# Layer norms in pairs, eight turns in one PSUM bank, and a new order for a two-layer attention and GLU kernel

## The chip, the cores and the metric

The kernel runs on one core of a Trainium2 chip. The metric is the device time of one execution in microseconds; the median of several runs is compared. The engines are named as in the profile: PE (TensorE, matmuls), PEld (its weight loads), DVE (VectorE), ACT (ScalarE), POOL (GpSimd) and SP (SyncE, which here issues most DMAs).

## The reference, cut to what matters

The input x has 2048 tokens of 512 numbers in bf16. Two layers are computed, with the same weights. Each has a sliding-window attention (32 heads of 16, window 256) and a gated feed-forward part (hidden size 1792), each on a layer norm of x and added to x:

```
def _layernorm(x, axis=-1, eps=1e-5):
    m = jnp.mean(x, axis=axis, keepdims=True)
    v = jnp.var(x, axis=axis, keepdims=True)
    return (x - m) / jnp.sqrt(v + eps)
...
    mask = (idx[:, None] - idx[None, :] >= 0) & (idx[:, None] - idx[None, :] < W)
    scores = jnp.where(mask[None, None], scores, -1e9)
    p = _softmax(scores, axis=-1)
    o = jnp.einsum("bhqk,bhkd->bhqd", p, v)
...
    h = _sigmoid(g) * u
    return jnp.einsum("bsf,fd->bsd", h, w_down)
...
x = x + _A_ref(_layernorm(x, axis=-1), A_wqkv, A_wo)
x = x + _B_ref(_layernorm(x, axis=-1), B_w_gate, B_w_up, B_w_down)
```

The last two lines are done twice. `A_x` is the input; `B_x` is not used.

## The kernel before, in words

The tokens are cut into 16 tiles of 128, and the tiles into four groups of four. x lies in SBUF for the whole run (`xsb`), and so do all weights.

**A norm.** `layer_norm` makes tasks for one tile. DVE takes the statistics (`stats`, L600 and L602), POOL adds epsilon and takes the inverse root (`root`, L612 and L613), DVE applies them (`apply`, L629) into a buffer `xn`, of which there are four, one tile each. PE turns the tile's four 128 x 128 blocks with the identity (L647) into one PSUM bank, as bf16, and ACT or DVE copies the bank (L676 is ACT's copy and L678 DVE's, both in a helper `copy`) into `xnT`, which holds a group of four tiles. There are 64 norms: per layer 16 for the attention (kind "p") and 16 for the feed-forward part (kind "g").

**The attention.** Q (L713), K (L744, with a split by VectorE at L759) and V (L780) are matmuls of a group or a tile. Scores go into four PSUM banks (`Sps`, L1039, L1050, L1060) in visits; each visit ends in one exponential on ACT of up to 128 x 2048 (L1092), and DVE multiplies with masks (L970). The values (L1119) go half a tile at a time into a bank; the result is moved to SBUF (`OTs`), transposed on DVE (`turn`, L1138), divided by the sums (`norm`, L1144 and L1146), and transposed back (`turn2`, L1151). The output projection (L903) adds to x (L909) and starts the feed-forward norm of the tile.

**The feed-forward part.** Tiles are taken in groups of 1, 2 or 4, in the lists `GLU`; `OPT["g0"]` picks the list of layer 0 (always followed by two groups of 4) and `OPT["g2"]` that of layer 1. A unit fills one bank with gate and up matmuls (L808; 128 columns wide for a group of one, 512 for four, where gate and up have a bank each), ACT takes the tanh (L826), DVE multiplies (L834), and the down projection (L872) ends with an addition to x on DVE (L881), which starts the next layer's norm or the store. Four PSUM banks (`BANKS`) are shared by all that isn't scores.

**The order.** It is fixed when the kernel is built. A planner written in Python keeps a clock, a queue of tasks for each engine and a list of open units for PE. A task has a duration in ns for each engine that can do it and a priority from `PRIO` (lower goes first); where two engines can do it, the one that would end it earlier takes it. A PE unit is chosen by `RANK`. `PACE` sets the least distance of score visits, with other values for the first `EARLY` visits, and from visit `PACE[4]` on `LATE_PRIO`, `LATE_RANK` and `LATE_SLACK` hold. The instructions are written out in the order in which the planner starts them, so each engine's own order is that of the plan, and the hardware waits with semaphores. The durations and priorities make no instruction longer or shorter; they set order and engine. In the plan, DVE's copy of a turned tile has 152 + 512/0.96 + 100 ns; the turn has 1130, the norm 1030, the second turn 600. When PE has nothing to do, the planner may put in idle-filling matmuls (L1257).

`OPT["bk"]` and `OPT["bq"]` are the numbers of first K and Q units that work tile by tile, 128 columns wide. `OPT["hold"]` makes the third and fourth norm wait for earlier ones. `OPT["g1"]` is used only by the changed kernel.

The lines that name the buffers and the tasks of a norm:

```
        ring("xn", 4, [P, 1, D])
...
        b = pl.task({"POOL": 800 - 230 * first}, root, [a.done], self.prio["st_" + kind])
        c = pl.task({"DVE": 406}, apply, [b.done], self.prio["ap_" + kind], can, port=True)
...
            d = pl.task({"ACT": act_ns(KT * P), "DVE": dve_ns(KT * P) + 100}, lambda e: self.copy(
                e, self.xnT[key][0][:, i], pt), [u.done], self.prio["tp" if key[0] == "p" else "tp_g"])
```

Of the kernel before, what the change touches and what calls it, by code (L numbers as in the profile page):

```python
# [9 lines left out]
ALU = mybir.AluOpType  # L10
# [34 lines left out]
def act_ns(n):  # L45
    return 171 + n / 1.2


def dve_ns(n):
    return 152 + n / 0.96  # L50
# [6 lines left out]
def pool_ns(n):  # L57
# [2 lines left out]

EXP_NS = 1880
TAIL = (384, 128)
GLU = [[[1, 1, 1, 1, 2, 2], [1, 1, 1, 1, 2, 2], [1, 1, 2, 2, 2], [1, 1, 1, 1, 1, 1, 1, 1], [2, 2, 2, 2], [1, 1, 1, 1, 1, 1, 1, 1], [2, 2, 4]], [[4, 4, 4, 4], [4, 4, 4, 2, 1, 1], [4, 4, 2, 1, 1, 4]]]
PACE = [2681.81, 1328.37, 1196.7, 872.42, 21.95]
EARLY = 16
FILL = 800
OVERLAP = {"ACT": 114, "DVE": 83, "POOL": 45, "SP": 0}
LATENCY = {"ACT": 45, "DVE": 40, "POOL": 60, "SP": 0}
# [11 lines left out]
FETCH = (1200, 2300)  # L80


PRIO = dict(st_x0=8.026, ap_x0=7.059, xt_x0=10.785, st_x1=3.545, ap_x1=6.693, xt_x1=8.977, st_x=12.044,
    ap_x=12.327, xt_x=-6.634, st_p=-1.733, ap_p=4.349, xt_p=1.138, st_g=-6.356, ap_g=3.74, xt_g=-5.594,
    st_g0=3.292, ap_g0=-10.915, xt_g0=-4.847, tp=7.272, tp_g=6.212, q=-0.67, q0=11.129, q1=-22.989,
    k=-9.747, k0=14.768, k1=0.61, s=-5.3, s0=4.016, s1=2.634, v=0.444, v0=23.378, v1=20.074, vv=-6.331,
    exp=-13.785, exp0=-0.049, m0=3.46, m00=4.795, e0=-8.802, e00=0.423, e1=-0.562, e10=9.011, m2=-6.041,
    m20=0.716, th=15.676, mu=-10.778, dn=-20.12, add=2.096, add0=7.831, out=-15.994, mv=31.961, mv0=5.964,
    oq=-8.579, oq0=-11.733, no=13.392, no0=-3.279, on=11.451, on0=-10.714, vc=11.541, vc0=-1.273)
OPT = dict(gu='SP', g1=0, bk=3, bq=3, wide=0, r0=2, g0=5, g2=0, x0=1, eps=1, hold=1, own=1, ck=0, cq=2,  # L90
    turn=2, split=0, mo=0, at=3, r1=3, near=3)
SLACK = dict(xt=5595, oq=812, on=1665, vc=730)
RANK = dict(tp=-16.462, o=-6.977, lead=17.162, far=65.44, v=20.015, g=58.528, d=32.436, feed=40.797,
    x3=34839.477, wd=1492.629, go=176.096)
LATE_PRIO = dict(st_p=-4.956, ap_p=38.034, xt_p=0.962, st_x=-1.619, ap_x=-5.199, xt_x=17.448, st_g=-14.573,
    ap_g=-6.614, xt_g=0.299, q=-17.247, k=34.931, s=-1.549, v=-6.237, exp=-43.312, m0=4.641, e0=8.453,
    e1=11.689, m2=17.496, th=2.747, mu=-20.998, dn=2.523, add=-6.022, out=27.029, mv=45.566, oq=-5.883,
    no=8.561, on=11.817, vc=-20.116)
LATE_SLACK = dict(xt=541, oq=5451, on=4000, vc=10531)
LATE_RANK = dict(tp=52.672, o=-17.659, lead=2.057, far=12.106, v=-5.627, g=-3.049, d=10.813, feed=-60.763,  # L100
    go=344.346)

# [28 lines left out]
def when_all(events, fn):  # L133
    left = [e for e in events if not e.fired]
    if not left:
        fn()
        return
    count = [len(left)]

    def one():  # L140
        count[0] -= 1
        if count[0] == 0:
            fn()

    for e in left:
        e.waiting.append(one)
# [226 lines left out]
class Net:  # L373


    def __init__(self, ctx, tc, A_x, wqkv, wo, w_gate, w_up, w_down, out):
# [41 lines left out]
        def ring(name, n, shape, dt=BF16):  # L418
            self.bufs[name] = [[big.tile(shape, dt, name=f"{name}{i}"), True] for i in range(n)]

        ring("xn", 4, [P, 1, D])
        ring("xnT", 3, [P, NBG, KT, P])
        ring("OTs", 1, [P, 8, P])
        ring("Oq", 1, [P, 8, P])
# [161 lines left out]
    def layer_norm(self, key, t, deps):  # L586

        nc, pl = self.nc, self.pl
        done = self.xn_ready[key, t]
        box = {}  # L590
        kind = "x" + ("0" if key[2] == 0 else "1" if key[2] == 1 else "") if key[:2] == ("p", 0) else (
            "p" if key[0] == "p" else "g0" if key[1] * NT + t < 4 else "g")

        first = key == ("p", 0, 0) and OPT["eps"]

        def stats(e):
            if "st" not in box:
                box["st"] = self.take("st")
            st = box["st"][0][:, 0]
            nc.vector.bn_stats(out=st[:, 0:6], in_=self.xsb[:, t, :])  # L600
            if not first:
                nc.vector.bn_aggr(out=st[:, 6:8], in_=st[:, 0:6])  # L602

        def moments(e):
            st = box["st"][0][:, 0]
            nc.vector.bn_aggr(out=st[:, 6:8], in_=st[:, 0:6])
            nc.vector.tensor_scalar(out=st[:, 9:10], in0=st[:, 7:8], scalar1=1e-5, scalar2=None, op0=ALU.add)

        def root(e):
            st = box["st"][0]  # L610
            if not first:
                nc.gpsimd.tensor_scalar(out=st[:, 0, 9:10], in0=st[:, 0, 7:8], scalar1=1e-5, scalar2=None, op0=ALU.add)  # L612
            nc.gpsimd.tensor_tensor(out=st[:, 0, 8:9], in0=st[:, 0, 9:10], in1=self.nhalf[:, 0:1], op=ALU.pow)  # L613

        def can():
            if not self.has("xn"):
                return False
            if key in self.xnT:
                return True
            room = sum(b[1] for b in self.bufs["xnT"])  # L620
            mine = sum(k[0] == key[0] for k in self.xnT)
            return room > 0 and (mine == 0 or room > 1 or key[:2] == ("p", 0))

        def apply(e):
            box["xn"] = b = self.take("xn")
            if key not in self.xnT:
                self.xnT[key] = self.take("xnT")
            st = box["st"][0][:, 0]
            nc.vector.tensor_scalar(out=b[0][:, 0, :], in0=self.xsb[:, t, :], scalar1=st[:, 6:7], scalar2=st[:, 8:9],  # L629
                                    op0=ALU.subtract, op1=ALU.mult)  # L630

        if key == ("p", 0, 0) and t >= 2 and OPT["hold"]:
            deps = deps + [self.applied[t - 2]]
        a = pl.task({"DVE": 694 if first else 910}, stats, deps, self.prio["st_" + kind], lambda: "st" in box or self.has("st"))
        if first:
            a = pl.task({"DVE": 390}, moments, [a.done] + ([self.applied[t - 1]] if 0 < t <= OPT["mo"] else []), self.prio["ap_" + kind] + 0.1)
        b = pl.task({"POOL": 800 - 230 * first}, root, [a.done], self.prio["st_" + kind])
        self.roots[key + (t,)] = b.done
        c = pl.task({"DVE": 406}, apply, [b.done], self.prio["ap_" + kind], can, port=True)
        c.done.then(lambda: self.give(box["st"]))  # L640
        if key == ("p", 0, 0):
            c.began_ev = self.applied[t]
        i = t % NBG
        def steps(bank):
            pt = self.tp_view(bank)
            xn = box["xn"][0][:, 0]
            return [(57, lambda c=c: nc.tensor.transpose(pt[:, c, :], xn[:, c * P:(c + 1) * P], self.ident[:]))  # L647
                    for c in range(KT)]

        def evac(u):  # L650
            pt = self.tp_view(u.bank)
            if key == ("p", 0, 0) and t < OPT["split"]:
                half, both = KT // 2, Event()
                when_all([pl.task({e: ns}, lambda e, o=o: self.copy(e, self.xnT[key][0][:, i][:, o:o + half], pt[:, o:o + half]), [u.done],
                                  self.prio["tp"] - 9).done for e, ns, o in (("ACT", act_ns(half * P), 0), ("DVE", dve_ns(half * P) + 50, half))], both.fire)
                both.then(lambda: (self.give(box["xn"]), done.fire()))
                return both
            d = pl.task({"ACT": act_ns(KT * P), "DVE": dve_ns(KT * P) + 100}, lambda e: self.copy(
                e, self.xnT[key][0][:, i], pt), [u.done], self.prio["tp" if key[0] == "p" else "tp_g"])
            d.done.then(lambda: (self.give(box["xn"]), done.fire()))  # L660
            return d.done

        def ready():
            u = Unit(("tp", t), steps, [], False, evac)
            if key == ("p", 0, 0) and OPT["own"]:
                u.own = BANKS + t
            self.streams[0].append(u)

        c.done.then(ready)

    def tp_view(self, bank, n=KT):
        return self.banks[bank][:, 0:n * P // 2].bitcast(BF16).rearrange("p (c q) -> p c q", c=n)
# [452 lines left out]
    def after_values(self, L, t, half, bank, done):  # L1125
# [29 lines left out]
        a.done.then(lambda: self.release(bank))  # L1155
        if half == 0:
            return
        b = pl.task({"DVE": 1130}, turn, [box[0], box[1]], self.prio["oq0" if early else "oq"], lambda: self.has("Oq"), port=True)
        b.done.then(lambda: self.give(box["OTs"]))
        c = pl.task({"DVE": 1030}, norm, [b.done], self.prio["no0" if early else "no"], lambda: self.has("On"), port=True)  # L1160
        c.done.then(lambda: (self.give(box["Oq"]), self.give(box["Rt"])))
        d = pl.task({"DVE": 600}, turn2, [c.done], self.prio["on0" if early else "on"], lambda: self.has("OnT"), port=True)

        def landed():
            self.give(box["On"])
# [321 lines left out]
```

## Time and profile before

| what | value |
|---|---|
| median of 3 runs | 565.57 us (565.51 to 566.4) |
| the profiled execution's own time | 566.81 us |
| its span, first to last instruction | 565.1 us |
| granted PE clock | 1.00 in all slices |
| ACT, exponentials (122 + 32) | 226.7 + 56.9 us |
| PE, gate and up matmuls | 125.7 + 125.6 us |
| DVE, feed-forward products (140) | 78.0 us |
| DMA | 17.38 MB, 31 GB/s on average |

The profile is of one execution. A row of a group reads: line, engine, operation, output <- inputs, shapes, count | busy time in us, mean ns of one | idle time of the engine just before them, and what ended it. A row of the stages gives the stretch in us from the span's start, its length, busy us (and count) of PE, PEld, DVE, ACT and POOL, the granted clock, the busy share of the DMA engines, and GB/s. A row of the waits gives who waited <- for whom: us in total, times, longest. A row of the timeline gives start, duration, engine, line, operation and count of merged instructions, and in brackets the idle time before it. Matmuls overlap, so the distance from start to start tells their rate, not the duration.

### The profile page before, as it was taken

The numbers are of one execution on the slowest core, as the hardware profiler recorded it, in microseconds if no ns is written. First come the engines' busy times: TensorE is split into PE (matmuls) and PEld (weight loads), VectorE is DVE, ScalarE is ACT, GpSimd is POOL, SyncE is SP. The second block draws the span as 40 slices with busy tenths as digits, with TensorE's granted clock in tenths as the row PEclk, the third lists the DMA queues.
The fourth block names the chain that finished last, engine by engine and source line by source line (L and its number), as shares of the span: only waits on it lengthen the run. The fifth ranks groups of instructions, "written<-read, shape, count | busy, mean of one in ns | idle before, by whom it ended". The sixth has DMA issues, their size and how long they took to land.

```text
span 565.1 us, 22076 instructions
## 1 busy us (share of the span) xinstructions
PE 548.7 (97%) x9998; PEld 300.0 (53%) x9998; DVE 461.9 (82%) x921; ACT 407.8 (72%) x424; POOL 61.4 (11%) x153
## 2 busy tenths in 40 slices
PE   8999899999999999999999999999999999999997
PEld 7446565854788645444444444544444444544443
DVE  6999999999988899996699986989768999852332
ACT  3999989979999887891699827999189985530330
POOL 4411111111101120101100011000100001000000
PEclk9999999999999999999999999999999999999999
DMA  8723000000000000000000000000100000000001
GB/s 254 294 92 106 3 24 2 23 3 23 4 23 3 23 3 23 23 2 1 11 2 23 3 13 11 2 23 3 40 20 2 23 3 31 12 1 20 19 0 38
DMA packets 18574, 17.38 MB, mean 31 GB/s; under 512 B 1841, under 2 KB 17457, under 8 KB 18481
## 3 DMA queue, kind: packets, MB, share of 16 engines
q1 hardware_dynamic: 17360, 14.93, 8.1%
q8 instruction: 78, 1.28, 0.9%
q10 hardware_dynamic: 1120, 1.05, 0.6%
q14 instruction: 16, 0.12, 0.1%
HBM read 9.70 MB, written 2.10 MB: 21 GB/s over the span
## 4 chain that ended last, share of the span: by engine, by line
PE 66%; DVE 21%; ACT 5%; issue 4%; DMA 2%; ACTq 1%; POOL 0%; SPq 0%; DVEq 0%
PE bank L808 29%; PE bank L872 14%; PE bank L1119 6%; PE Sps L1039 5%; PE bank L903 5%; DVE PTring L970 3%; DVE kTp L759 3%; PE bank L713 2%; DVE Oq L1138 2%; PE bank L780 2%; DVE edge L970 2%; ACT PTring L1092 2%; DVE On L1146 2%; DVE st L600 1%; DMA wg<-in_B_w_gate_dram 1%
## 5 line engine op out<-in xcount | busy, mean ns | idle before, releaser
L1092 ACT ACTIVATE PTring<-Sps 128x2048 bf16<-128x2048 f32 (+1 forms) x122 | 226.7, 1859 | 29.2 <-PE Sps L1039 26.6
L808 PE MATMUL bank<-xnT,wg 128*128 128x128 bf16 (+1 forms) x784 | 125.7, 288 | 1.3 <-ACT xnT L676 0.9
L808 PE MATMUL bank<-xnT,wu 128*128 128x128 bf16 (+1 forms) x784 | 125.6, 288 | 0.0
L872 PE MATMUL bank<-wd,hT 128*128 128x512 bf16 (+2 forms) x462 | 103.3, 373 | 0.0
L834 DVE SCALAR_TENSOR_TENSOR hT<-hT,bank 128x512 bf16<-128x512 bf16 (+1 forms) x140 | 78.0, 570 | 27.0 <-PE bank L808 23.1
L826 ACT ACTIVATE hT<-bank 128x512 bf16<-128x512 f32 (+1 forms) x140 | 69.3, 518 | 33.3 <-PE bank L808 33.1
L808 PEld LDWEIGHTS <-wg 128*128 128x128 bf16 x784 | 58.9, 98 | 40.4 <-issue 4.0
L808 PEld LDWEIGHTS <-wu 128*128 128x128 bf16 x784 | 59.1, 98 | 38.3 <-issue 2.3
L872 PEld LDWEIGHTS <-hT 128*128 128x128 bf16 x462 | 42.9, 98 | 49.2 <-issue 1.6
L612 POOL TENSOR_SCALAR st<-st 128x1 f32<-128x1 f32 x60 | 17.8, 297 | 426.1 <-DVE st L602 426.0
L1092 ACT ACTIVATE edge<-Sps 128x2048 bf16<-128x2048 f32 (+1 forms) x32 | 56.9, 1777 | 8.8 <-PE Sps L1050 8.1
L676 ACT COPY xnT<-bank 128x512 bf16<-128x512 bf16 x36 | 20.1, 603 | 46.4 <-PE bank L647 46.4
L1119 PE MATMUL bank<-PTring,Vaug 128*32 128x64 bf16 (+1 forms) x2880 | 52.5, 203 | 0.7 <-DVE PTring L970 0.5
L1039 PE MATMUL Sps<-qT,kTp 32*128 32x256 bf16 (+3 forms) x1216 | 47.5, 248 | 3.7 <-ACT PTring L1092 1.9
L1119 PEld LDWEIGHTS <-Vaug 128*32 128x32 bf16 x2880 | 44.1, 97 | 13.1 <-issue 11.1
L600 DVE BATCH_NORM_STATS2 st<-xsb 128x6 f32<-128x512 bf16 x64 | 43.7, 683 | 2.6 <-DMA xsb<-in_A_x_dram 2.2
L1119 PE MATMUL bank<-edge,Vl 128*32 128x64 bf16 x1024 | 44.2, 193 | 0.9 <-DVE edge L970 0.7
L881 DVE SCALAR_TENSOR_TENSOR xsb<-bank,xsb 128x512 bf16<-128x512 f32 (+2 forms) x33 | 22.0, 665 | 28.1 <-PE bank L872 28.0
L970 DVE TENSOR_TENSOR PTring<-PTring,mask 128x1024 bf16<-128x1024 bf16 x64 | 43.3, 678 | 1.2 <-ACT PTring L1092 1.0
L1039 PEld LDWEIGHTS <-kTp 32*128 32x128 bf16 x1216 | 18.8, 92 | 44.1 <-issue 41.1
L1138 DVE STREAM_TRANSPOSE Oq<-OTs 128x1024 bf16<-128x1024 bf16 x32 | 39.7, 1240 | 1.6 <-ACT OTs L676 1.0
L1119 PE MATMUL bank<-edge,Vh 128*32 128x64 bf16 x896 | 40.8, 193 | 0.0
(70 smaller groups left out, 691.0 us busy)
## 6 DMA issues: line engine op xcount, KB each, us to landing
Vl<-Vaug SPq DMA_DIRECT2D x32, 68.0 KB, 2.2
out_dram<-xsb SPq DMA_DIRECT2D x15, 128.0 KB, 2.1
Vh<-Vaug SPq DMA_DIRECT2D x28, 68.0 KB, 2.2
wg<-in_B_w_gate_dram SPq DMA_DIRECT2D x2, 896.0 KB, 9.2
wu<-in_B_w_up_dram SPq DMA_DIRECT2D x2, 896.0 KB, 11.8
wd<-in_B_w_down_dram SPq DMA_DIRECT2D x7, 256.0 KB, 3.7
xsb<-in_A_x_dram SPq DMA_DIRECT2D x6, 256.0 KB, 5.7
wq<-in_A_wqkv_dram SPq DMA_DIRECT2D x3, 256.0 KB, 5.7
```

Of the source, the lines that this page charges most:

```text
L600: nc.vector.bn_stats(out=st[:, 0:6], in_=self.xsb[:, t, :])
L808: return [(mm_ns(w), lambda i=i, j=j, fc=fc, wt=wt, kt=kt: self.nc.tensor.matmul(pt[:, i, j, :], lhsT=wt[:, kt, fc * P:(fc + 1) * P], rhs= ...
L826: self.nc.scalar.activation(out=self.hT[:, ch[0] * GW:ch[0] * GW + size], in_=pt, func=AF.Tanh, scale=0.5)
L834: self.nc.vector.scalar_tensor_tensor(out=h, in0=h, scalar=1.0, in1=pt, op0=ALU.add, op1=ALU.mult)
L872: nc.tensor.matmul(self.banks[bank][:, 0:w], lhsT=self.hT[:, at:at + P], rhs=self.wd[:, fc, d], start=fc == 0, stop=fc == FC - 1)
L881: e = pl.task({"DVE": dve_ns(w)}, lambda e: nc.vector.scalar_tensor_tensor(out=self.xsb[:, t, d], in0=self.banks[u.bank][:, 0:w], scalar=0 ...
L903: return [(mm_ns(D), lambda c=c: nc.tensor.matmul(self.banks[bank][:], lhsT=b[0][:, c, :], rhs=self.wot[:, c, :], start=c == 0, stop=c == ...
L970: done = pl.task({"DVE": dve_bf_ns(1024)}, lambda e: nc.vector.tensor_tensor(out=r, in0=r, in1=m.to_broadcast([P, 16, HP]), op=ALU.mult), ...
L1039: nc.tensor.matmul(self.sps[:, m, o:o + n * HP], lhsT=kTp[32 * m:32 * m + 32, i, tt, e, :], rhs=self.qT[32 * m:32 * m + 32, i, q0:q0 + n * ...
L1092: nc.scalar.activation(out=out, in_=src, func=AF.Exp, scale=scale)
L1119: nc.tensor.matmul(o, lhsT=Va[:, c0:c0 + 32], rhs=p(h), start=k == 0 or t == 0, stop=k == len(parts) - 1 or t == 0, tile_position=(0, 32 * g))
L1138: nc.vector.transpose(out=box["Oq"][0][:].rearrange("p c q -> p (c q)"), in_=box["OTs"][0][:].rearrange("p c q -> p (c q)"))
```

## The change

Norms are now made for two neighbouring tiles together, except the first four of layer 0's attention and the first two of its feed-forward part, which stay alone. The statistics and the application are still one instruction a tile on DVE. The inverse root on POOL serves both tiles with one pair of instructions and waits for the statistics of both. `xn` has two buffers of two tiles. PE's eight turns of a pair go into one PSUM bank, and one copy of 128 x 1024 on ACT or DVE takes them to `xnT`. The plan has new durations for DVE's copies (425 and 670), turn (1260), norm (1230) and second turn (725). All the numbers that set the order are new, the choice of groups among them: layer 0 takes `GLU[0][1]` and layer 1 `GLU[1][1]`.

```
-GLU = [[[1, 1, 1, 1, 2, 2], [1, 1, 1, 1, 2, 2], [1, 1, 2, 2, 2], [1, 1, 1, 1, 1, 1, 1, 1], [2, 2, 2, 2], [1, 1, 1, 1, 1, 1, 1, 1], [2, 2, 4]], [[4, 4, 4, 4], [4, 4, 4, 2, 1, 1], [4, 4, 2, 1, 1, 4]]]
-PACE = [2681.81, 1328.37, 1196.7, 872.42, 21.95]
-EARLY = 16
+GLU = [[[1, 1, 1, 1, 2, 2], [1, 1, 2, 1, 1, 2], [1, 1, 2, 2, 2], [1, 1, 1, 1, 2, 1, 1], [2, 2, 2, 2], [1, 1, 1, 1, 1, 1, 1, 1], [2, 2, 4]], [[4, 4, 2, 1, 1, 1, 1, 2], [4, 4, 4, 2, 2], [4, 4, 2, 1, 1, 4]]]
+PACE = [2666.65, 1903.85, 2579.89, 2302.59, 11.33]
+EARLY = 4
...
-OPT = dict(gu='SP', g1=0, bk=3, bq=3, wide=0, r0=2, g0=5, g2=0, x0=1, eps=1, hold=1, own=1, ck=0, cq=2,
-    turn=2, split=0, mo=0, at=3, r1=3, near=3)
+OPT = dict(gu='SP', g1=0, bk=1, bq=1, wide=0, r0=2, g0=1, g2=1, x0=1, eps=1, hold=0, own=1, ck=0, cq=2,
+    turn=2, split=0, mo=0, at=3, r1=0, near=2)
...
-        ring("xn", 4, [P, 1, D])
+        ring("xn", 2, [P, 2, D])
...
+        alone = key[:2] == ("p", 0) and t < NBG * (1 + OPT["g1"]) or key[0] == "g" and key[1] * NT + t < 2
...
-            nc.gpsimd.tensor_tensor(out=st[:, 0, 8:9], in0=st[:, 0, 9:10], in1=self.nhalf[:, 0:1], op=ALU.pow)
+            nc.gpsimd.tensor_tensor(out=st[:, 0:n, 8:9], in0=st[:, 0:n, 9:10], in1=self.nhalf[:, 0:n].rearrange("p (n x) -> p n x", x=1),
+                                    op=ALU.pow)
...
+            for k, tt in enumerate(tiles):
+                st = box["st"][0][:, k]
+                nc.vector.tensor_scalar(out=b[0][:, k, :], in0=self.xsb[:, tt, :], scalar1=st[:, 6:7], scalar2=st[:, 8:9],
+                                        op0=ALU.subtract, op1=ALU.mult)
...
+        if not alone:
+            box["ready"].append(a.done)
+            if len(box["ready"]) < 2:
+                return
...
-            d = pl.task({"ACT": act_ns(KT * P), "DVE": dve_ns(KT * P) + 100}, lambda e: self.copy(
+                d = pl.task({"ACT": act_ns(KT * P), "DVE": 425}, lambda e: self.copy(
...
+            def steps(bank):
+                pt = self.tp_view(bank, 2 * KT)
+                xn = box["xn"][0][:].rearrange("p t d -> p (t d)")
+                return [(57, lambda c=c: nc.tensor.transpose(pt[:, c, :], xn[:, c * P:(c + 1) * P], self.ident[:]))
+                        for c in range(2 * KT)]
+
+            def evac(u):
+                d = pl.task({"ACT": act_ns(2 * KT * P), "DVE": 670}, lambda e: self.copy(
+                    e, self.xnT[key][0][:, i:i + 2].rearrange("p t c q -> p (t c) q"), self.tp_view(u.bank, 2 * KT)),
+                    [u.done], self.prio["tp" if key[0] == "p" else "tp_g"])
...
-        b = pl.task({"DVE": 1130}, turn, [box[0], box[1]], self.prio["oq0" if early else "oq"], lambda: self.has("Oq"), port=True)
+        b = pl.task({"DVE": 1260}, turn, [box[0], box[1]], self.prio["oq0" if early else "oq"], lambda: self.has("Oq"), port=True)
...
-        c = pl.task({"DVE": 1030}, norm, [b.done], self.prio["no0" if early else "no"], lambda: self.has("On"), port=True)
+        c = pl.task({"DVE": 1230}, norm, [b.done], self.prio["no0" if early else "no"], lambda: self.has("On"), port=True)
...
-        d = pl.task({"DVE": 600}, turn2, [c.done], self.prio["on0" if early else "on"], lambda: self.has("OnT"), port=True)
+        d = pl.task({"DVE": 725}, turn2, [c.done], self.prio["on0" if early else "on"], lambda: self.has("OnT"), port=True)
```

`PRIO`, `RANK`, `SLACK` and their `LATE_` forms have other numbers throughout.

## The prediction

> **What bounds the kernel now.** I read the page's head first, then the busy times by stage, then the waits, and last the groups with their shapes.
>
> ```profile
> span 565.1 us, 22076 instructions
> PE 548.7 (97%) x9998; PEld 300.0 (53%) x9998; DVE 461.9 (82%) x921; ACT 407.8 (72%) x424; POOL 61.4 (11%) x153
> ```
>
> The stages I cut myself: the start, the part of layer 0 in which the attention runs ahead, the rest of layer 0, layer 1's interleaved part, and the feed-forward tail.
>
> ```profile
> 0.00:14.00 14.00, 11.69 (x162) 11.23 (x162) 8.91 (x38) 5.45 (x9) 6.25 (x25) 1.00 0.84 254
> 14.00:113.00 99.00, 93.47 (x2048) 59.15 (x2046) 94.51 (x205) 91.86 (x100) 18.73 (x48) 1.00 0.23 78
> 113.00:254.00 141.00, 139.07 (x3260) 84.13 (x3258) 131.49 (x265) 124.38 (x130) 15.81 (x33) 1.00 0.05 13
> 254.00:494.00 240.00, 237.91 (x4211) 114.61 (x4209) 201.16 (x376) 170.70 (x162) 19.36 (x46) 1.00 0.04 13
> 494.00:565.00 71.00, 66.60 (x327) 30.88 (x325) 25.83 (x42) 15.41 (x26) 1.29 (x3) 1.00 0.05 15
> ```
>
> The columns are length, then PE, PEld, DVE, ACT and POOL busy, clock, DMA. From 254 on PE is open for 2.1 us of 240, and DVE and ACT have room. From 14 to 113 it is otherwise: PE is open for 5.5 us of 99, and DVE (95%) and ACT (93%) are nearly as full. That is the only long stage in which cheaper copies or a truer order can move the end by much.
>
> A busy PE need not be a needed PE, so I worked out its demand from the rates in a piece of the timeline:
>
> ```profile
> 100.74 0.40 PE L1039 MATMUL Sps<-qT,kTp 32*128 32x256 bf16 x8
> 101.07 0.27 PE L1119 MATMUL bank<-PTring,Vaug 128*32 128x128 bf16 x8
> ...
> 101.88 0.34 PE L808 MATMUL bank<-xnT,wu 128*128 128x128 bf16 x3
> 102.05 0.61 PE L808 MATMUL bank<-xnT,wg 128*128 128x128 bf16 x8
> 102.50 0.61 PE L808 MATMUL bank<-xnT,wu 128*128 128x128 bf16 x8
> ```
>
> From start to start a score visit takes 0.33 us, a half tile of values 0.81, and a 128-column matmul 0.45/8 = 0.056. In the tail eight 512-column ones start every 1.72 us, 0.215 each. The groups have 1594 matmuls of 512 columns (343 us), 1248 of 128 with the turns (70), 4800 of values, 80 to a half tile (49), and 154 score visits (one per exponential, 51): 513 us. The start costs some 9 us over its useful work and the end 3.4 after the last matmul. About 40 are left; returning from scores or values to dense work costs near 0.1 each in such pieces, 20 or so for 214 returns. So an order can win back perhaps 15 to 20 us at the very best, and the waits that the trace names on PE itself are much smaller (waits of PE, 14 to 113):
>
> ```profile
> PE Sps L1039 <- ACT PTring L1092: 1.9, 4, 0.8
> PE Sps L1039 <- ACT edge L1092: 1.5, 3, 0.6
> PE bank L647 <- DVE Vaug L678: 0.6, 1, 0.6
> PE bank L780 <- DMA wg<-in_B_w_gate_dram: 0.5, 1, 0.5
> ```
>
> What ends last there is ACT's exponential, which keeps its place in a queue filled up with copies and evacuations.
>
> **The change part by part.** The rows:
>
> ```profile
> L676 ACT COPY xnT<-bank 128x512 bf16<-128x512 bf16 x36 | 20.1, 603 | 46.4 <-PE bank L647 46.4
> L678 DVE COPY xnT<-bank 128x512 bf16<-128x512 bf16 x24 | 9.3, 415 | 0.4 <-PE bank L647 0.3
> L1138 DVE STREAM_TRANSPOSE Oq<-OTs 128x1024 bf16<-128x1024 bf16 x32 | 39.7, 1240 | 1.6 <-ACT OTs L676 1.0
> L1151 DVE STREAM_TRANSPOSE OnT<-On 128x512 bf16<-128x512 bf16 x32 | 22.6, 706 | 0.0
> ```
>
> *Copies.* Six of 64 norms stay alone, 58 become 29 pairs. ACT's gate activation takes 598 at 512 columns and 396 at 256: 0.79 ns a column, so a pair's copy is 603 + 404 = 1007 ns against 1206, 199 saved. On DVE a 512-column f32 eviction is 685 and its 256-to-512 slope 1.04, so its fixed part is about 151; the 415 of the bf16 copy leaves 0.52 a column, a pair 679 against 830, 151 saved. All 29 pairs: 4.4 to 5.8 us of engine time. On the path counts only the stage 14 to 113, where 16 of the 64 copies stand (9 on ACT, 7 on DVE): about 7 pairs, 1.1 to 1.4 us. As it can fall beside a full DVE or beside a wait of another kind, its worth is 0 to 1.4; I take 0.8.
>
> *One bank for eight turns.* PE's turns are the same 256. The Trainium skill (PSUM — Partial Sum Buffer, "PSUM bank collisions raise a hardware error") states that ScalarE and VectorE may not read one bank in the same partitions at once. Two tiles in two banks can be copied by ACT and DVE side by side (0.60 us in all); in one bank one engine has to do both (0.68 to 1.01), and by the rule each exposed pair is 0.1 to 0.4 us later. Where PE is seen to wait for these copies, in the tail, the trace does otherwise:
>
> ```profile
> 523.65 0.61 PE L647 MATMUL bank<-ident,xn 128*128 128x128 bf16 x8
> ...
> 524.07 1.07 ACT L676 COPY xnT<-bank 128x512 bf16<-128x512 bf16 x2 [12.58 <-PE bank L647]
> 525.20 1.02 PE L808 MATMUL bank<-xnT,wg 128*128 128x512 bf16 x4 [0.94 <-ACT xnT L676]
> ```
>
> Both go over ACT, one behind the other, so there a pair costs nothing more. By the rule at four exposed places the sum would be 1.6 worse; by the row 0. I take the row.
>
> *POOL.* 297 + 602 ns a tile become about as much a pair (one or two elements a lane): 26 us less on an engine that is 11% busy and waits for DVE (426 us). Worth nothing but a shorter queue; if a root were on a path, it would be 0.9 us later only as the second tile is.
>
> *The order.* The plan thinks 1130 for the first turn, 1030 for the norm, 600 for the second turn; the rows say 1240, 342 + 2 x 422 = 1186, and 706. Each attention tile holds DVE 110 + 156 + 106 = 372 ns longer than planned; six stand in 14 to 113 (2.2 us) and eleven in 113 to 254 (4.1). The other way, it books a copy on DVE at 785 ns that takes 415 (24 x 370 = 8.9 us), which sends copies to ACT that DVE would have done in two thirds of the time. An order made with true durations should put the exponentials' inputs and PE's work where they are ready. It cannot take more than PE's open 5.5 us and 1.9 us in the two stages plus some of the stretched returns; and a new order makes waits of its own, so its worth is bounded by -7 and, from below nothing, +5. I take a third of the open time: 1.8 + 0.6.
>
> *Feed-forward groups.* In layer 0 eight single tiles become four singles and two groups of two. A single costs 4 x 0.056 = 0.225 a 512-column step against 0.215, 4.6%. The four tiles that move are 448 matmuls of 128 columns, 25.1 us; with 256 columns, for which no row exists, they cost 24.1 (as 512) to 25.1. I take 24.3, so 0.8 saved. Layer 1 cuts its last four tiles into 2 + 2: 0 to 1.1 us lost by the same bounds, 0.3 taken. ACT and DVE there go from 14 steps of 598 and 677 to 28 of 396 and 410, 2.7 and 2.1 us more, beside 24 us of PE work: hidden.
>
> *Tail, start.* The gap of 0.94 before the last group may go or, with two groups, occur twice: -0.9 to +0.9, zero taken. At the start the K and Q units done tile by tile fall from three each to one: the others are then 512 wide, but begin only when tile 3 is turned. Before its copy ends at 11.65 PE does 26 narrow K and Q matmuls; one unit of each offers 24 by then (three tiles of four steps): -0.3 to +1, zero taken. The loads are unchanged.
>
> Sum: -0.8 - 1.8 - 0.6 - 0.8 + 0.3 = -3.7. The profiled execution's own time is 566.8, 1.7 over its span; so 563.1 for it, and 561.9 beside the median of 565.57.
>
> **The rivals.**
> *Pairs starve PE (slower).* A norm now waits for its neighbour. Around 58 us the trace shows how thin the supply is: PE does three turns one by one as xn comes, waits 0.34 for DVE, runs four idle-filling matmuls, then waits 0.76 for an exponential. The o-projections up to 84 us stand one to each 14 us window; the first tile of a pair is held for such a pitch. One tile of feed-forward work is 112 x 0.056 = 6.3 us plus 14 x 0.215 = 3.0. If in layer 0's early part PE lacks half of it (4.7 us), the work is done later, at 226 to 268, where PE has no opening, so all of it is added: near 569 (561.9 + 4.7, and the reorder's 2.4 not gained). It decides once PE is open for over 9 us between 14 and 113. Against it: Q, K and V work of the next groups fills too, and six norms stay alone.
> *The engines off the path get the gain (no change).* PE's named waits in the middle are short; if freed ACT and DVE time only lengthens their own waits, N=256 and the second group cancel, 565.6.
> *The order repairs more.* If all 5.5 and 1.9 us are recovered and the tail's gap too, with the copies' 0.8 and the groups' 0.5: 565.6 - 9.6 = 556 to 558.
>
> **How the numbers follow.** This kernel's runs agree within about 0.2%, 1.1 us, which is also what can be told from no change. The likeliest, 561.9 (own range 559 to 564.3), has 0.43; more repaired, about 557, 0.15; no change 0.13; starved, 566.8 to 572, 0.29, because the whole order is new and PE has little to win and anything to lose. Faster 0.58, same 0.13, slower 0.29. From 557 to 570 leaves out half of the better case and a third of the worse one.
>
> **What would show it.** Right: xnT copies of 1024 columns near 1.0 us on ACT and 0.68 on DVE, PE's open time between 14 and 113 at 3 to 4 us, unchanged matmul rates, and the last group's start without a longer wait. Wrong: idle-filling matmuls after 14 us beyond the present eight; PE waiting for xnT or xn in layer 0 for over 2 us; a longer score pitch; or 256-column matmuls above 0.112 us each. The prediction fails if the new order spends PE's time in more returns between scores, values and dense work.

## The result and the profile after

The changed kernel takes 561.08 us (median of 4 runs, 560.89 to 561.27) against 565.99 for the one before in the same comparison: 0.9913 of it, 95% interval 0.9900 to 0.9925. That is 4.9 us less, where 3.7 were forecast. The profiled span is 559.2 us, 5.9 less. The profiled execution of the kernel before was one of its slower ones (566.81 us, 0.8 over the median) and that of the changed kernel was not (560.94), so about 1 us of the 5.9, and of the differences read from the two traces below, is scatter between executions.

First the head of the page, after:

```profile
span 559.2 us, 21591 instructions
PE 540.1 (97%) x9788; PEld 303.6 (54%) x9846; DVE 464.5 (83%) x927; ACT 404.9 (72%) x417; POOL 41.0 (7%) x95
```

58 matmul records are missing against PEld's count; most likely that is why 2.5 us of PE's waits, in all, stand as "issue" below. POOL's work fell by 20.4 us. ACT's copies into `xnT` fell by 15.6 us and DVE's rose by 6.5, but other evacuations and narrower feed-forward steps took most of that room: in all ACT's work fell by 2.9 and DVE's rose by 2.6. The groups of the pairs' copies and of POOL's power, after:

```profile
L705 ACT COPY xnT<-bank 128x1024 bf16<-128x1024 bf16 x6 | 6.0, 1011 | 21.2 <-PE bank L688 21.2
L707 DVE COPY xnT<-bank 128x1024 bf16<-128x1024 bf16 x23 | 15.1, 682 | 0.0
L620 POOL TENSOR_TENSOR st<-st,nhalf 128x2 f32<-128x2 f32 (+1 forms) x35 | 24.4, 697 | 7.4 <-DVE st L613 4.8
```

The two copies cost 1011 and 682 ns, forecast as 1007 and 679. DVE does 23 of the 29 pairs; before it did 24 of the 64 single copies.

Where the time went is seen from equal marks in both timelines. The 37th exponential, before and then after:

```profile
114.51 1.88 ACT L1092 ACTIVATE PTring<-Sps 128x2048 bf16<-128x2048 f32 x1
```

```profile
111.46 1.91 ACT L1121 ACTIVATE PTring<-Sps 128x2048 bf16<-128x2048 f32 x1
```

The twelfth of the 16 feed-forward additions of layer 0, the first close mark behind 254, before and after:

```profile
271.79 0.69 DVE L881 SCALAR_TENSOR_TENSOR xsb<-bank,xsb 128x512 bf16<-128x512 f32 x1 [2.33 <-PE bank L872]
```

```profile
267.59 0.69 DVE L910 SCALAR_TENSOR_TENSOR xsb<-bank,xsb 128x512 bf16<-128x512 f32 x1 [1.39 <-PE bank L901]
```

So 3.05 us are won up to 111 and 1.15 more up to this mark. By the addition before the tail's first store (514.79 before, 508.68 after) another 1.9 are won, half of them before layer 0's last addition (340.93 and 335.79), while layer 1's attention runs beside it; the tail loses 0.3. Counted by PEld's loads and the matmuls' widths, the same dense work lies before the three marks in both kernels, but for up to eight turns.

A gain can come from PE waiting less or from PE being busy for less time with the same work. From 14 to the first mark, before and then after (length, then PE, PEld, DVE, ACT, POOL, clock, DMA):

```profile
14.00:114.51 100.51, 94.98 (x2085) 60.35 (x2086) 95.23 (x207) 93.37 (x103) 18.85 (x48) 1.00 0.22 77
```

```profile
14.00:111.46 97.46, 92.90 (x1964) 57.07 (x1979) 94.79 (x204) 91.98 (x98) 12.56 (x25) 1.00 0.23 77
```

PE's open time there fell by 1.0 (5.5 to 4.6) and its busy time by 2.1. Over the whole run PE is open for 16.4 us before and 19.1 after; without the 2.5 of "issue" that is no change. The gain as a whole lies in PE's busy time: 548.7 against 540.1, or 542.6 if those 2.5 are counted as work. The waits of PE over the whole run, after:

```profile
PE bank L837 <- DVE xnT L707: 2.1, 6, 0.6
PE bank L809 <- DVE xnT L707: 1.5, 3, 0.7
PE bank L901 <- issue: 1.4, 9, 0.2
PE Sps L1068 <- ACT PTring L1121: 1.3, 4, 0.5
PE bank L661 <- DVE xn L638: 1.1, 1, 1.1
```

PE waits 3.6 us for xnT in nine places. Before it was 1.6 in three (0.9 for ACT's copy in the tail; 0.5 and 0.2 in the rest of layer 0). The waits for exponentials fell, 3.4 to 1.3 between 14 and 113. The waits that the trace names were therefore traded, not removed, and the traces alone don't show which part of the change earned the time.

### The profile page after: what moved, and what is told of

Its sections match the earlier page's. It is cut to its first block, busy times and chain, and to the rows that moved or that the text cites. A ratio compares the mean times of both kernels' runs of the same rounds, so it can differ in the third digit from the quotient of the medians.

```text
span 559.2 us, 21591 instructions
## 1 busy us (share of the span) xinstructions
PE 540.1 (97%) x9788; PEld 303.6 (54%) x9846; DVE 464.5 (83%) x927; ACT 404.9 (72%) x417; POOL 41.0 (7%) x95
## 3 DMA queue, kind: packets, MB, share of 16 engines
q10 hardware_dynamic: 1120, 1.05, 0.6%
## 4 chain that ended last, share of the span: by engine, by line
PE 76%; DVE 17%; issue 3%; ACT 3%; POOL 0%; DMA 0%; SPq 0%; ACTq 0%; DVEq 0%; POOLq 0%
PE bank L837 32%; PE bank L901 17%; PE bank L1148 7%; PE Sps L1068 5%; PE bank L932 4%; PE bank L742 4%; PE bank L809 3%; DVE kTp L788 3%; DVE PTring L999 2%; DVE edge L999 1%; DVE xnT L707 1%; ACT PTring L1121 1%; PE Sps L1079 1%; DVE st L606 1%; PE bank L1286 1%
## 5 line engine op out<-in xcount | busy, mean ns | idle before, releaser
L837 PE MATMUL bank<-xnT,wu 128*128 128x512 bf16 (+2 forms) x728 | 129.6, 298 | 0.0
L837 PE MATMUL bank<-xnT,wg 128*128 128x512 bf16 (+2 forms) x728 | 127.2, 297 | 2.2 <-DVE xnT L707 2.1
L855 ACT ACTIVATE hT<-bank 128x256 bf16<-128x256 f32 (+1 forms) x154 | 71.0, 488 | 47.2 <-PE bank L837 46.4
L901 PE MATMUL bank<-wd,hT 128*128 128x512 bf16 (+2 forms) x440 | 100.4, 373 | 2.1 <-issue 1.4
L863 DVE SCALAR_TENSOR_TENSOR hT<-hT,bank 128x256 bf16<-128x256 bf16 (+1 forms) x154 | 80.0, 534 | 21.9 <-ACT hT L855 16.4
L837 PEld LDWEIGHTS <-wg 128*128 128x128 bf16 x728 | 61.8, 98 | 38.8 <-issue 4.9
L837 PEld LDWEIGHTS <-wu 128*128 128x128 bf16 x728 | 61.0, 98 | 33.8 <-issue 3.6
L619 POOL TENSOR_SCALAR st<-st 128x2 f32<-128x2 f32 (+1 forms) x31 | 11.1, 359 | 448.5 <-DVE st L608 448.5
L999 DVE TENSOR_TENSOR edge<-edge,maske 128x1024 bf16<-128x1024 bf16 x60 | 40.2, 675 | 0.1
```

The costliest lines, as they stand in the source:

```text
L837: return [(mm_ns(w), lambda i=i, j=j, fc=fc, wt=wt, kt=kt: self.nc.tensor.matmul(pt[:, i, j, :], lhsT=wt[:, kt, fc * P:(fc + 1) * P], rhs= ...
L855: self.nc.scalar.activation(out=self.hT[:, ch[0] * GW:ch[0] * GW + size], in_=pt, func=AF.Tanh, scale=0.5)
L863: self.nc.vector.scalar_tensor_tensor(out=h, in0=h, scalar=1.0, in1=pt, op0=ALU.add, op1=ALU.mult)
L901: nc.tensor.matmul(self.banks[bank][:, 0:w], lhsT=self.hT[:, at:at + P], rhs=self.wd[:, fc, d], start=fc == 0, stop=fc == FC - 1)
L999: done = pl.task({"DVE": dve_bf_ns(1024)}, lambda e: nc.vector.tensor_tensor(out=r, in0=r, in1=m.to_broadcast([P, 16, HP]), op=ALU.mult), ...
```

## The experiments

Two theories stand against each other. The prediction's: truer durations make a better order (2.4 us), cheaper copies and wider groups give the rest. The rival's: the numbers that set the order are fitted to one plan, and what is compared is one fitted set with another. Ratios are against the kernel before, each in its own comparison.

**e1, the same order, two copies for one.** In the changed kernel, one task of the plan emits both copies:

```
-  lambda e: self.copy(e, self.xnT[key][0][:, i:i + 2]..., self.tp_view(u.bank, 2 * KT))
+  lambda e: [self.copy(e, self.xnT[key][0][:, i + k], self.tp_view(u.bank, 2 * KT)[:, k * KT:k * KT + KT, :]) for k in range(2)]
```

> The changed kernel with its order kept instruction for instruction, but each pair's copy out of the bank done as two copies of 512 columns one behind the other on the same engine, in the place of the one of 1024. It isolates the copy's own worth. Theory of the prediction: 0.15 us (DVE) to 0.2 us (ACT) more in each of 29 pairs, 4.4 to 5.8 us of engine time, of which 0.8 us reaches the end: 561.1 + 0.8 = 561.9, at most 1.4 more. Rival (the single copy is what pairs are for, and it is the main gain): 563.5 to 565. Rival (copies are off the path): within 0.3 of 561.1.

560.64 us, 0.9899 (0.9886 to 0.9913): not to be told from the changed kernel, and not slower. Its copies:

```profile
L707 DVE COPY xnT<-bank 128x512 bf16<-128x512 bf16 x46 | 16.6, 415 | 0.0
L705 ACT COPY xnT<-bank 128x512 bf16<-128x512 bf16 x14 | 7.5, 592 | 21.2 <-PE bank L688 21.2
```

ACT and DVE kept their order, instruction for instruction, with two copies in the place of each one (two of ACT's 14 belong to single norms). So each pair did cost the 150 to 170 ns that had been saved, and the end didn't see it. The rival "off the path" holds; the prediction's 0.8 us is not there in this order.

**e2, single norms; e3, old durations; e4, only new durations.** Each takes one part of the change away, or does one alone, and the order is planned anew.

```
e2, from the changed kernel:
-  alone = key[:2] == ("p", 0) and t < NBG * (1 + OPT["g1"]) or key[0] == "g" and key[1] * NT + t < 2
+  alone = True
-  ring("xn", 2, [P, 2, D])
+  ring("xn", 4, [P, 1, D])
e3, from the changed kernel: turn 1130, norm 1030, second turn 600, copies dve_ns(n) + 100
e4, from the kernel before:  turn 1260, norm 1230, second turn 725, copy 425
```

> The changed kernel with every norm alone again and four one-tile buffers, all other numbers (durations, priorities, groups) as changed; the order is planned anew from them. If the pairs give only their copies (prediction): 0.5 to 1.5 us slower than the changed kernel, 561.6 to 562.6. If the pairs are the main gain: 564 to 566. If the priorities are fitted to one plan and any replanning loses (rival): 563 to 567, with more waits in places that have nothing to do with norms.

> The changed kernel, pairs, priorities and groups kept, with the plan's durations as before (turn 1130, norm 1030, second turn 600, DVE copies by the old formula, 785 and 1319). Theory of the prediction, that the true durations are the largest term (2.4 us): 563 to 564.5, with more copies on ACT and PE's open time between 14 and 113 up by 2. If durations matter little: 560.6 to 561.6. If any replanning loses: 563 to 567.

> The kernel before with only the new durations in the plan (turn 1260, norm 1230, second turn 725, DVE copy of one tile 425), its priorities, groups and single norms kept; the order is planned anew. Theory of the prediction: 1.5 to 2.5 us faster than before, 563.5 to 564.5. If the priorities are fitted to one plan and any replanning loses: 566.5 to 570. If durations matter little: 565.5 to 566.5.

582.64 us, 1.0286 (1.0267 to 1.0304); 583.42, 1.0302 (1.0284 to 1.0319); 580.68, 1.0255 (1.0239 to 1.0270). All three lose 14 to 22 us, more than any theory had asked of its own part. e4 is the hardest against the prediction: truer durations alone, which were to save some 2 us, cost 14.2 (580.68 against 566.48 in its comparison). No part of the change has such a price in its rows, so the loss was looked for in the order itself.

**e5, e6, e7: ten nanoseconds.** These change one planned duration by 10 ns. No instruction's own work changes.

```
e5, from the changed kernel:  norm 1230 -> 1240
e6, from the kernel before:   turn 1130 -> 1140
e7, from the changed kernel:  turn 1260 -> 1250
```

> The changed kernel with one number of the plan moved by 10 ns (the norm's duration 1240 instead of 1230); no instruction is longer or shorter, only the order is planned anew. Theory A (what the three replanned kernels lost, they lost because the priorities are fitted to one plan, and the new order is a draw): 5 to 20 us slower than 561.1, with layer 0's last visits or layer 1's first moved by tens of us against the feed-forward groups. Theory B (the replanned kernels lost because singles or false durations are worse in themselves): 560.5 to 562, since 10 ns are nothing.

> The kernel before with one number of its plan moved by 10 ns (the turn's duration 1140 instead of 1130), nothing else. Theory A (fitted priorities): 10 to 25 us slower than before, 576 to 591, though the number is nearer to the measured 1240. Theory B: 565 to 567.

> The changed kernel with the turn's planned duration 1250 instead of 1260. Theory A allows any draw; where no group of the feed-forward part changes its place against the visits, small differences stay: 561 to 563.5. Theory B: 560.5 to 562.

577.65 us, 1.0203 (1.0186 to 1.0220); 596.66, 1.0542 (1.0526 to 1.0558); 561.74, 0.9927 (0.9913 to 0.9942). Ten nanoseconds cost 16.6 and 30.7 us, in e6 although the number came nearer to the truth. The third draw cost 0.7, less than can be told from nothing. So a run that plans anew with the same numbers says almost nothing of the part that it takes away: e2, e3 and e4 fall under this.

The trace shows what happens. Busy time in stretches of 14 us (columns as above), the changed kernel:

```profile
352.00:366.00 14.00, 13.90 (x258) 6.66 (x258) 12.95 (x25) 12.89 (x13) 0.00 (x0) 1.00 0.01 3
366.00:380.00 14.00, 14.00 (x364) 6.86 (x349) 11.92 (x22) 13.11 (x12) 0.00 (x0) 1.00 0.08 22
...
408.00:422.00 14.00, 13.71 (x206) 6.55 (x204) 9.82 (x21) 12.21 (x12) 0.00 (x0) 1.00 0.04 12
422.00:436.00 14.00, 13.95 (x272) 6.47 (x271) 11.76 (x21) 12.85 (x13) 0.00 (x0) 1.00 0.01 2
```

And e5:

```profile
352.00:366.00 14.00, 14.00 (x66) 6.37 (x65) 5.69 (x9) 4.78 (x8) 0.00 (x0) 1.00 0.00 1
366.00:380.00 14.00, 14.00 (x81) 6.29 (x79) 3.80 (x7) 1.14 (x3) 0.00 (x0) 1.00 0.11 36
...
408.00:422.00 14.00, 9.23 (x318) 5.17 (x311) 11.23 (x23) 11.78 (x10) 1.57 (x2) 0.82 0.08 23
422.00:436.00 14.00, 12.88 (x174) 5.38 (x173) 9.50 (x17) 8.96 (x8) 0.00 (x0) 0.69 0.01 2
```

Read ACT first. In e5 the plan works off a four-tile feed-forward group between 338 and 380 with no attention visits beside it: ACT has 1 to 5 us of 14 to do, PE is full, nothing seems wrong. No exponential starts between 324.16 and 379.93; the 108th, which the changed kernel starts at 341.45, is the next. But that dense work was the filler for the visits that follow. From 380 to 450 ACT is busy for 59.6 us of 70 and PE for only 61.5; of the 8.5 that PE is open, it waits 5.1 for exponentials, and its granted clock falls to 0.69 in a stretch. A part of e5's timeline in which PE waits:

```profile
413.75 0.62 PE L1068 MATMUL Sps<-qT,kTp 32*128 32x256 bf16 x8 [2.00 <-ACT edge L1121]
...
419.37 0.40 PE L1068 MATMUL Sps<-qT,kTp 32*128 32x256 bf16 x8 [1.45 <-ACT PTring L1121]
421.84 0.50 PE L688 MATMUL bank<-ident,xn 128*128 128x128 bf16 x3 [0.54 <-DVE xn L638]
```

Against the changed kernel PE is open 7.0 us more between 380 and 450 (61.5 busy against 68.5). In this stretch it is busy for 11.8 us at half clock (the rows stand in the last section); if all of that work takes twice its time, as its 512-column matmuls do (0.43 us each from start to start), 5.9 of it are added. By this estimate the two make 13 of the 16.5 us by which the span grew. In e3 and e6 whole stretches of the same kind stand too (ACT 4.8 us of 14 at 352 in e3, at 282 in e6). Tens of us of visits move; the loss comes where the filler is gone.

**e8, other groups in layer 1.** `OPT["g2"]` is 0 instead of 1, which takes the list 4, 4, 2, 1, 1, 1, 1, 2. (The expectation begins as if the last group kept four tiles; the list that it names is what ran.)

> The changed kernel with layer 1's last feed-forward group left at four tiles (the list 4, 4, 2, 1, 1, 1, 1, 2 stands in the place of 4, 4, 4, 4, so the groups 2, 1, 1, 1, 1, 2 follow the first two fours): narrower matmuls for eight tiles instead of four. By matmul rates alone: the 256-column rate is 0.109 us against 0.1075 for half of a 512, so four tiles at 256 and four at 128 columns cost about 0.7 us of PE more than 4, 2, 2: 561.8. By theory A, order effects on top: 562 to 565.

563.57 us, 0.9957 (0.9942 to 0.9972), 2.5 over the changed kernel. All 154 exponentials start within 0.5 us of the changed kernel's or earlier, so the loss is in the tail. There is no upheaval here. Of the loss about 1.0 is width (448 matmuls of 128 columns, 25.1 us, for 112 of 512, 24.1), and 0.9 is PE waiting for xnT from 478 on, 1.4 us against 0.5. The 0.7 expected for the width was too low by its own rates; some 0.6 us of the loss are not explained.

**e9 to e12: each combination with its own fit.** If the fit decides, each combination of norms and durations needs its own. The numbers of the order, the choice of groups and the switches of the start among them, were searched for each of the four with some 13,000 random steps from the two known sets, judged by the end of the kernel's own plan. For example e9, cut to what is short enough to show:

```
-GLU = ... [1, 1, 2, 1, 1, 2] ... [4, 4, 4, 2, 2] ...
-PACE = [2666.65, 1903.85, 2579.89, 2302.59, 11.33]
-EARLY = 4
+GLU = [[[1, 1, 1, 1, 2, 1, 1]], [[4, 4, 4, 4]]]
+PACE = [2018.5204283757303, 858.5553917371467, 299.55094635173145, 120.45251799886219, 10.148662498724043]
+EARLY = 16
```

> The changed kernel (pairs, new durations) with the numbers that set the order (priorities, ranks, slacks, pace, the choice of groups) searched once more, some 13,000 random steps from the kernels' own two sets, each judged by the end of the kernel's own plan; instructions of a task are unchanged. Its plan ends at 550.4 (the changed kernel's at 559.1, and its span was 559.2). If the time is set by the fit of the numbers (theory A) and the plan tells it truly: a span of 550 to 553, 552 to 555 us. If the search only exploits the plan's errors: 558 to 565.

> Single norms with the new durations, searched in the same way and for as long; its plan ends at 552.0. Theory A (neither pairs nor copies matter, the fit does): within 2 us of the searched pairs, 553 to 556. If pairs are worth something of themselves: 3 us or more slower than the searched pairs, although the numbers were fitted to them.

> The kernel before (single norms, old durations) with its numbers searched in the same way and for as long; its plan ends at 555.8. If true durations matter only through the plan's truth: the span runs over its plan by 2 to 4 us (before: plan 562.8, span 565.1), 558 to 562 us, so slower than the searched kernel with single norms and new durations by 3 to 6. If durations don't matter: within 2 us of that one.

> Pairs with the old durations, searched in the same way and for as long; its plan ends at 560.5. If the plan is optimistic with old durations: 563 to 567. If old durations are as good as new: 561.5 to 563.

| run | norms, durations | plan's end | span | time | ratio (95%) |
|---|---|---|---|---|---|
| e9 | pairs, new | 550.4 | 551.2 | 552.61 | 0.9767 (0.9752 to 0.9781) |
| e10 | single, new | 552.0 | 554.4 | 556.23 | 0.9830 (0.9815 to 0.9844) |
| e11 | single, old | 555.8 | 557.0 | 559.10 | 0.9887 (0.9871 to 0.9904) |
| e12 | pairs, old | 560.5 | 562.8 | 564.45 | 0.9972 (0.9963 to 0.9982) |

Three things follow. Singles with the *old* durations, the kernel before with other numbers, win 6.7 us, more than the whole change: so a gain of this size needs neither pairs nor new durations. With equal search the new durations come out better with both kinds of norms (2.9 us for singles, 11.8 for pairs). Pairs come out better with new durations (3.6) and worse with old (5.4), so they have no clear sign. It is one search for each, and how far two searches of the same kind differ was not measured; a few us may be luck. And e9 beats both kernels, 8.5 us under the changed one. The shares of the chain that ended last, after and then e9:

```profile
PE 76%; DVE 17%; issue 3%; ACT 3%; POOL 0%; DMA 0%; SPq 0%; ACTq 0%; DVEq 0%; POOLq 0%
```

```profile
PE 84%; DVE 10%; issue 2%; ACT 2%; POOL 1%; DVEq 0%; ACTq 0%; POOLq 0%
```

The chain passes over DVE for 10% of the span instead of 17%.

## Why the prediction was right, and where its steps were wrong

**The stage and the bound: right.** The gain was to come mostly between 14 and 113 (2.6 forecast, from copies and order; 3.05 measured at the mark at 111) and from 113 to 254 (0.6 and 0.8 forecast, 1.15 measured at the mark behind it). PE remained the bound. That the sum came so near is in part luck: the 0.8 forecast for the copies didn't come, 1.6 came after 254, where 0.3 were to be lost, and the same reasoning gave a gain for e4, which lost 14.2.

**Where PE's time was to come from: wrong.** The order's worth was taken as a third of PE's open time, and the sign named for it was an open time of 3 to 4 us between 14 and 113. It is 4.6. Over the whole run PE's open time did not fall at all, and what shrank is its busy time for the same work, of which the widths explain 0.3. The prediction named this term ("some of the stretched returns") and gave it no price. Which of PE's work got shorter is not shown. Most of its other signs came out: four idle-filling matmuls after 14 us where there had been eight, and a shorter wait at the last groups. PE's waits for xn and xnT in layer 0, with 2 us as the sign against it, are 1.7 from 14 to 254 and another 0.6 in the start.

**The order by truer durations, 2.4 us: the amount came, the reason was not shown.** The prediction said that "an order made with true durations should put the exponentials' inputs and PE's work where they are ready". e4 gave true durations to the old numbers and lost 14.2. By exclusion the change's gain is that of its new order: the copies are worth nothing by e1 and the widths 0.3 by their rates, while POOL's fewer instructions were not tested alone. The new order comes from a second set of numbers with new durations together; e11 shows that a set fitted to the old durations can win more. That truer durations make a better target for the fit is suggested by e9 against e12 and e10 against e11, and by the plan: with old durations the kernel before runs 2.3 us over its plan (562.8 planned, span 565.1), with new ones the changed kernel 0.1 (559.1, 559.2). But e10 runs 2.4 over, so even that is not settled.

**The copies, 0.8 us: wrong, 0.** Their sizes are within 4 ns; e1 shows that in this order they are off the path. POOL's pair is not "about as much" as a single (356 + 717 ns against 297 + 602), so 20.4 us went there and not 26.

**One bank for two tiles: open.** The tail's row said that nothing is lost, and the rule on bank collisions that the prediction cites 1.6 us at four places. In the tail, where the row was taken, the wait for xnT fell from 0.94 to 0.49 us; over the whole run PE's waits for xnT rose by 2.0 us, to nine places. That the shared bank is the cause is not shown: a test, two copies on two engines, would need a second bank and was not tried. e9, with pairs too, has only 0.9 us of such waits between 14 and 113 and none of 0.2 or more after, so an order can hide them.

**Groups: right in size.** A 256-column matmul starts every 0.109 us, four in 0.437, as the tail shows:

```profile
519.09 0.60 PE L837 MATMUL bank<-xnT,wg 128*128 128x256 bf16 x4 [0.49 <-DVE xnT L707]
519.52 0.60 PE L837 MATMUL bank<-xnT,wu 128*128 128x256 bf16 x4
519.96 0.60 PE L837 MATMUL bank<-xnT,wg 128*128 128x256 bf16 x4
```

So four tiles cost 24.5 where I took 24.3; by these rates 0.7 us are won in layer 0 and 0.4 lost in layer 1.

**After 254: wrong by 1.9.** I had +0.3 for layer 1's groups and nothing else; 1.9 were won before the tail, which lost 0.3. Up to 1 of it may be scatter between the two profiled executions. PE's small waits there were seen, but the time that its work is stretched between visits was thought fixed.

**The rival "pairs starve PE": its mechanism is real, its cause another.** Starvation after filler was worked off too early is what e5 shows. There it came from the order of the groups, not from a tile that waits for its neighbour. I gave it one price, near 569; the draws of the order ran to 597. I looked for it in layer 0's early part, and it was layer 1 that showed it.

## What to carry to other kernels

Where a planner with fitted priorities writes the order, taking one part of a change away and planning anew tests the plan and not the part: move one number by an amount that cannot matter first, and see how far the time goes. A part is measured alone only if the order is kept (as in e1), and a combination is judged only after its own fit, more than once. In the trace, look for long dense work with an idle ACT: its price is paid later, where the visits have no filler left.

## What was not expected of the hardware

PE's granted clock fell to half although no wait was over 2.0 us. In e5 it changed at 413.65, 417.07, 420.48 and 430.72 us: each change after the first comes 3.41 us, or three times that, after the one before. Stretches of e5 cut at these times (PE busy first, the clock the third number from the end):

```profile
406.83:410.24 3.41, 3.41 (x100) 1.77 (x98) 3.27 (x10) 3.30 (x4) 0.00 (x0) 1.00 0.08 24
410.24:413.65 3.41, 1.05 (x35) 0.48 (x34) 3.38 (x7) 3.35 (x3) 0.00 (x0) 1.00 0.22 63
413.65:417.07 3.42, 3.22 (x94) 1.76 (x97) 2.35 (x4) 2.55 (x3) 0.00 (x0) 0.50 0.03 7
417.07:420.48 3.41, 1.74 (x62) 0.79 (x62) 2.45 (x5) 2.54 (x2) 0.72 (x2) 1.00 0.00 0
420.48:423.89 3.41, 2.51 (x76) 1.59 (x62) 2.77 (x5) 2.10 (x2) 0.85 (x1) 0.50 0.00 0
423.89:427.31 3.42, 2.66 (x37) 1.04 (x37) 3.38 (x8) 2.47 (x2) 0.00 (x0) 0.50 0.02 5
427.31:430.72 3.41, 3.41 (x16) 0.98 (x15) 2.11 (x4) 0.88 (x2) 0.00 (x0) 0.50 0.00 0
430.72:434.13 3.41, 3.41 (x99) 1.77 (x100) 2.11 (x4) 2.85 (x3) 0.00 (x0) 1.00 0.00 0
```

The clock fell after stretches in which PE was busy for 1.05 and 1.74 us of 3.41, stayed at half after 2.51 and 2.66, and came back after 3.22 and 3.41. The Trainium skill (TensorE: Matmul & The Clock Gate, "What's actually happening") names an idle window of about 3.4 us for the fall and a busy one for the return. The length and the return agree; the fall came here after windows in which PE worked for a third and for half of the time. The share at which it turns is not shown.
